# Moving eleven stationary tiles by 32 to 448 bytes inside their slots, in a fused linear-attention and gMLP kernel

## The chip, the core and the metric

The kernel runs on one core of a Trainium2 chip. The metric is the device time of one execution in microseconds (us); the time before is the median of three runs.

## What is computed

The input `x` has 2048 rows of 512. It is normalized by rows, and two branches are added to it:

```python
xn = _layernorm(x, axis=-1)
return x + _A_ref(xn, A_wqkv, A_w_phi, A_wo) + _B_ref(xn, B_w_in, B_w_sp, B_b_sp, B_w_out)

# A: linear attention, 32 heads of 16
qkv = (x @ wqkv)...; pq = q @ w_phi; pk = k @ w_phi            # per head
phi_q = [softmax(pq), softmax(-pq)]; phi_k = [softmax(pk), softmax(-pk)]
kv = phi_k^T v; z = sum_s phi_k
o = (phi_q kv) / (phi_q z + 1e-6);  return o @ wo

# B: gMLP
z = gelu(x @ w_in)                     # 512 -> 1376
z1 = z[..., :688]; z2 = layernorm(z[..., 688:])
g = w_sp @ z2 + b_sp                   # over the 2048 rows
return (z1 * g) @ w_out
```

All arrays are float32.

## The kernel before

The 2048 rows are 16 tiles of 128 (`NT`, index `s`). For exactness with fast matmuls every operand is split into a rounded part and a remainder: ScalarE rounds (`round_h`, line 49), VectorE subtracts (`rest_l`, line 53), and `mm3` (lines 57 to 59) makes three matmuls of each product: high by high, high by low, low by high. The first operand of a matmul is the stationary one: TensorE loads it with a weight load of its own (the engine row PEld in the profile), 128 columns at a time; the second is the moving one, which streams past.

The centered and transposed x of a tile is `xT[s]`: 128 partitions, 2 x 512 values, first the rounded part, then the remainder. It is the stationary operand of all products with x: of `proj` (512 moving columns: wv, and the two halves of wqk, whose matrix is folded with w_phi) and of `zproj`, which `z1_raw` calls for z1 with the weights `w1`, and the z2 stage with `w2` (twice 344 moving columns each). One tile's z1 (12) runs in 512 and 176 columns instead, and so does tile 0's z2. An `xT` tile is read up to the end of the z2 stage, some 150 us or more after it was written.

The stages in order of time: the projections, the softmax features and z1 (to about 216 us; the last z1 tiles, 11 to 15, behind the other projections), z2 (to 276), the gate products `g` (to 480; a Strassen form with moving operands `B` from z2 and stationary operands `A` from w_sp, 344 columns, also through `mm3`), then the output projections `pout`. A scheduler sets the order inside the projection stage; the rest stands as written.

All `xT` tiles come from the pool `xz`: 16 slots, each `SL` = 1408 values long, that is 5632 bytes or eleven times 512. The pool begins 448 bytes past a multiple of 512, and so do the weights `wv`, `wqk`, `w1` and `w2`, whose pieces of one contraction step are 2048 or (padded from 344 to 384 columns) 1536 bytes apart. Of a slot, an `xT` tile takes the first 4096 bytes. Before and after it the slots hold other things (raw weights, `xc`, later `B` and others), at addresses that the change leaves alone. A `B` tile has four blocks of 344 values, 1376 bytes apart, in the same kind of slot; the `A` tiles begin at 448 or 0 past a multiple of 512.

Two places make an `xT` tile: `split_x`, for tiles 1 to 15, and a piece of code of its own for tile 0.

Of the kernel before, what the change touches and what calls it, by code (L numbers as in the profile page):

```python
# [11 lines left out]
F32R = mybir.dt.float32r  # L12
# [7 lines left out]
S, D, H, DH, FH = 2048, 512, 32, 16, 688  # L20
# [21 lines left out]
def mixer(ctx: ExitStack, tc: tile.TileContext, x, x_t, wv, wqkT, phi_bd, wo, w_in, wst, b_r, w_out, out):  # L42
# [4 lines left out]
    def round_h(eng, h, src):  # L47
        if eng is act:
            return act.activation(h, src, AF.Copy).ins  # L49
        return eng.tensor_copy(h, src).ins  # L50

    def rest_l(l, src, h, eng=None):
        return (eng or dve).tensor_tensor(l, src, h.bitcast(F32), op=ALU.subtract).ins  # L53
# [18 lines left out]
    def xz_tile(n, dt, name):  # L72
        return xz.tile([P, SL], dt, tag="xz", name=name)[:, :n]
# [64 lines left out]
    def zproj(ps, s, w, order=(0, 1), wide=False):  # L138

        if ps in (za, kv_ps_p):  # L140
            p = [ps.tile([P, D], F32, tag="z", name="zps") for _ in range(2)]
        else:
            q = ps.tile([P, 2, D], F32, tag="z", name="zps")
            p = [q[:, k] for k in range(2)]
        t = xT[s]
        if wide:
            parts = [(slice(0, 2), slice(LW, FC)), (slice(0, 2), slice(0, LW))]
            dst = [p[k][:, :2 * (f.stop - f.start)].rearrange("p (a b) -> p a b", a=2) for k, (_, f) in enumerate(parts)]
            for (_, f), d in zip(parts, dst):
                for c in range(ND):  # L150
                    cs = slice(c * P, (c + 1) * P)
                    zproj.last = mm3(d, (t[:, 0, cs], t[:, 1, cs]), [v[:, :, c, f] for v in w.both], c == 0, c == ND - 1)
            return list(zip(parts, dst))
        for k, j in enumerate(order):
            for c in range(ND):
                cs = slice(c * P, (c + 1) * P)
                zproj.last = mm3(p[k][:, :FC], (t[:, 0, cs], t[:, 1, cs]), (w[j][0][:, c], w[j][1][:, c]), c == 0, c == ND - 1)
        if ps in (za, kv_ps_p):
            return [((slice(k, k + 1),), p[k][:, :FC].unsqueeze(1)) for k in range(2)]
        return [((slice(0, 2),), q[:, :, :FC])]  # L160
# [7 lines left out]
    def z1_raw(pl, ps, s, bufs, wide=False):  # L168
        z = pl.tile([P, 2, FC], F32, tag="zf", bufs=bufs, name="z1f")
        for k, p in zproj(ps, s, w1, wide=wide):  # L170
            act.activation(z[(slice(None), *k)], p, AF.Copy, scale=r_x[:, s:s + 1])
        act.dma_start(z1_d[s], z.rearrange("p a b -> p (a b)"))

    LAG = 5
    RUNS = (3, 7, 11, 13, 15)
    xT = []
    ctx_w1 = left("w1", 1)
# [17 lines left out]
    with ExitStack() as p0:  # L195
# [60 lines left out]
        def load_win(dst, j):  # L256
            t = zw.tile([P, 4, FC], F32, tag="z2", bufs=2, name="wst_")
            for c in range(ND):
                split_w(dst[0][:, c], dst[1][:, c], w_in[c * P:(c + 1) * P, j * FC:(j + 1) * FC], t[:, c])
# [12 lines left out]
                xt[s] = load_x(s)  # L272

        def split_x(src):
            t = xz_tile(2 * D, F32R, "xT").rearrange("p (a b) -> p a b", a=2)
            xT.append(t)
            rounded.append(round_h(act, t[:, 0], src))
            split_x.last = rest_l(t[:, 1], src, t[:, 0])
            return rounded[-1], split_x.last
# [21 lines left out]
        def centered(s):  # L301
            stats(s)
            nm = neg_mean(s)
            rstd_of(mv_x[:, s], r_x[:, s:s + 1])
            with tc.issue_after(rounded[s - 2]):
                center(s, nm)
            split_x(transposed(s)[0])
# [36 lines left out]
        def proj_v(s):  # L344
            keep_v(s, proj(s, wv_h, wv_l))
# [12 lines left out]
        def add_kv(s, er):  # L358
# [4 lines left out]
            ready.append((v.pop(s), e))  # L363
            if s not in RUNS:
                return
            first = s == RUNS[0]
            with ExitStack() as later:
# [59 lines left out]
        def split_t(pt):  # L427
            i, j = split_x(pt)
            keep(act=i, dve=j)


        t = xz_tile(2 * D, F32R, "xT").rearrange("p (a b) -> p a b", a=2)
        xT.append(t)
        x0, pts = xt.pop(0), []
        for k in range(2):
            pts.append(ps.tile([P, 2, P], F32, tag="mm", name="pt"))
# [14 lines left out]
        p = ps.tile([P, D], F32, tag="mm", name="proj")  # L451
# [7 lines left out]
        p = ps.tile([P, D], F32, tag="mm", name="proj")  # L459
# [18 lines left out]
        p = ps.tile([P, D], F32, tag="mm", name="proj")  # L478
# [19 lines left out]
        ek.append(proj_k(1))  # L498
        keep(pe=proj.last)
        split_x(turned(3))  # L500
        z1_raw(wk, za, 0, 2)
        keep(pe=zproj.last)
# [3 lines left out]
        for s in range(NT):  # L506
# [26 lines left out]
            elif 2 < s < NT - 1:  # L533
                proj_v(s + 1)
            while n1 < s * (NT - LAG) // (NT - 1):
                z1_raw(wk, za, n1, 2)
# [95 lines left out]
    with ExitStack() as p1:  # L632
# [6 lines left out]
        def make_zb():  # L639

            ones_r = tmp1.tile([P, P], F32R, name="ones_r")
            round_h(act, ones_r, ones)
            for k in range(2):
                pz = psk.tile([P, D], F32, tag="kvt", name="pz")
                cs = slice(k * D, (k + 1) * D)
                h, l = (zhl[:, 2 * k + n] for n in range(2))
                round_h(act, h, zacc[:, cs])
                rest_l(l, zacc[:, cs], h)
                pe.matmul(pz, ones_r, h, start=True, stop=False)
                pe.matmul(pz, ones_r, l, start=False, stop=True)  # L650
                dve.tensor_copy(zb[:, cs], pz)
# [13 lines left out]
        for j in range(2):  # L665
            load_win(w2[j], 2 + j)
        for s in range(NT - LAG, NT):
            z1_raw(tmp1, (za, zbp)[s % 2], s, 2, s == NT - LAG + 1)
            if s == NT - LAG + 2:
                make_zb()  # L670
# [67 lines left out]
    for s in range(NT):  # L738
        p = zproj((kv_ps_p, zc, zbp, za)[s % 4], s, w2, (0, 1) if s % 2 == 0 else (1, 0), s == 0)
# [147 lines left out]
    for n in range(NC):  # L887
# [13 lines left out]
        if n % NQ == NQ - 1 and i < NP - 1:  # L901
# [3 lines left out]
            if i in (2, 4):  # L905
                s = i // 2 - 1
                e, t = (gt.tile([P, 2, FU], F32, tag=tag, name=name).rearrange("p k f -> p (k f)")[:, :NF]
                        for tag, name in (("c", "c"), ("z1", "z1t")))
# [12 lines left out]
        if n == NC - 2:  # L921
# [4 lines left out]
            t = xz_tile((KF + 1) * P, F32R, "u1")  # L926
# [156 lines left out]
    p, nxt = {}, dict(enumerate(uT))  # L1083
# [62 lines left out]
```

## Time and profile before

| | |
|---|---|
| median of 3 runs | 616.13 us (615.02 to 616.36) |
| the profiled execution | 618.88 us |
| its span, first to last instruction | 617.1 us |
| granted TensorE clock | 0.997 |
| TensorE busy | 606.7 us |
| VectorE busy | 518.9 us |
| ScalarE busy | 261.3 us |

PE is TensorE's matmuls, PEld its weight loads, DVE is VectorE, ACT ScalarE, POOL GpSimd, SP the engine that issues most transfers. Rows of a group give line, engine, operation, names out<-in, and xcount. A matmul's recorded end is modelled; consecutive matmuls overlap, so that the distance from start to start (called the pace here) is shorter than the recorded duration. In windows, an instruction counts in a window that it touches with any part.

### The profile page before, as it was taken

What the parts mean: (1) busy time and instruction counts of PE and PEld (TensorE: products, weight loads), DVE (VectorE), ACT (ScalarE), POOL (GpSimd) and SP (SyncE); (2) the same over time, 40 slices, a digit from 0 to 9 for tenths busy, and PEclk for the clock granted to TensorE, in tenths of its full rate; (3) what the DMA queues carried; (4) which work ended last, traced back from release to release, by engine and by line L of the source; (5) the groups of instructions that cost most, each with busy time, mean ns of one, the idle gap of its engine ahead of it and who ended that gap; (6) DMA issues with size and microseconds to landing.
All of it is one profiled execution on the core that took longest, in us unless ns stands there. A gap on an engine that the chain in (4) does not pass through costs nothing.

```text
span 617.1 us, 11396 instructions
## 1 busy us (share of the span) xinstructions
PE 606.7 (98%) x4286; PEld 552.5 (90%) x4286; DVE 518.9 (84%) x929; ACT 261.3 (42%) x416; POOL 134.7 (22%) x236
## 2 busy tenths in 40 slices
PE   8999999999999999999999999999999998999996
PEld 6888888888888999999999999999999886777775
DVE  5999999999978588999899897697879889799921
ACT  5653334323523547886444443343345232332221
POOL 4123232232110024452000002001000222143420
PEclk9999999999999999999999999999999998999999
DMA  8557876666447848001463646446466799799782
GB/s 312 191 136 169 224 178 174 158 160 172 125 140 201 287 144 302 2 1 35 151 150 114 199 118 193 129 128 192 135 184 224 202 330 363 216 276 245 191 219 58
DMA packets 58414, 109.95 MB, mean 178 GB/s; under 512 B 12456, under 2 KB 24616, under 8 KB 58120
## 3 DMA queue, kind: packets, MB, share of 16 engines
q1 hardware_dynamic: 43400, 64.96, 34.4%
q0 software_dynamic: 12656, 38.64, 24.9%
q10 hardware_dynamic: 2304, 5.64, 2.4%
q8 instruction: 33, 0.54, 0.4%
q14 instruction: 21, 0.17, 0.1%
HBM read 66.85 MB, written 35.80 MB: 166 GB/s over the span
## 4 chain that ended last, share of the span: by engine, by line
PE 89%; DMA 5%; DVE 3%; issue 2%; SPq 1%; ACT 0%; POOL 0%; POOLq 0%; DVEq 0%
PE g L57 11%; PE g L59 11%; PE g L58 11%; PE proj L58 7%; PE proj L57 7%; PE proj L59 7%; PE zps L59 6%; PE zps L58 6%; PE zps L57 6%; PE pout L57 4%; PE pout L59 4%; PE pout L58 4%; DMA zacc<-e 1%; DMA er<-et 1%; PE kvps L373 1%
## 5 line engine op out<-in xcount | busy, mean ns | idle before, releaser
L57 PE MATMUL g<-B,A 128*128 128x344 f32 x448 | 142.6, 319 | 0.0
L58 PE MATMUL g<-B,A 128*128 128x344 f32 x448 | 142.3, 319 | 0.0
L59 PE MATMUL g<-B,A 128*128 128x344 f32 x448 | 139.4, 319 | 0.0
L57 PEld LDWEIGHTS g<-B,A 128*128 128x128 f32 x448 | 84.0, 188 | 0.3 <-ACT A L49 0.3
L58 PEld LDWEIGHTS g<-B,A 128*128 128x128 f32 x448 | 84.1, 188 | 0.0
L59 PEld LDWEIGHTS g<-B,A 128*128 128x128 f32 x448 | 83.6, 188 | 0.0
L49 ACT ACTIVATE A<-S 128x512 fp32r<-128x512 f32 x64 | 39.2, 628 | 74.3 <-DVE S L622 49.6
L57 PE MATMUL proj<-wqk_h,xT 128*128 128x512 f32 x128 | 50.1, 391 | 0.0
L59 PE MATMUL proj<-wqk_h,xT 128*128 128x512 f32 x128 | 49.8, 389 | 0.0
L58 PE MATMUL proj<-wqk_l,xT 128*128 128x512 f32 x128 | 49.8, 389 | 0.0
L125 ACT ACTIVATE e<-e,r_x 128x1024 f32<-128x1024 f32 x26 | 29.8, 1148 | 42.2 <-DVE e L124 41.2
L53 DVE TENSOR_TENSOR A<-S,A 128x512 fp32r<-128x512 f32 x64 | 42.8, 683 | 3.0 <-ACT A L49 2.8
L49 ACT ACTIVATE A<-wf 128x512 fp32r<-128x512 f32 (+1 forms) x64 | 32.8, 517 | 25.2 <-DMA wf<-in_wst 14.2
L57 PE MATMUL zps<-w1h,xT 128*128 128x344 f32 (+2 forms) x128 | 40.7, 320 | 0.0
L58 PE MATMUL zps<-w1l,xT 128*128 128x344 f32 (+2 forms) x128 | 40.7, 318 | 0.0
L59 PE MATMUL zps<-w1h,xT 128*128 128x344 f32 (+2 forms) x128 | 40.7, 318 | 0.0
L57 PE MATMUL zps<-w2h,xT 128*128 128x344 f32 (+2 forms) x128 | 40.7, 318 | 0.0
L58 PE MATMUL zps<-w2l,xT 128*128 128x344 f32 (+2 forms) x128 | 40.6, 317 | 0.0
L59 PE MATMUL zps<-w2h,xT 128*128 128x344 f32 (+2 forms) x128 | 40.3, 317 | 0.0
L53 DVE TENSOR_TENSOR A<-wf,A 128x512 fp32r<-128x512 f32 (+1 forms) x64 | 34.8, 548 | 4.9 <-ACT A L49 4.8
L128 DVE TENSOR_REDUCE sm<-e 128x64 f32<-128x1024 f32 x26 | 31.1, 1198 | 2.5 <-ACT e L125 2.5
L787 POOL DMA_DIRECT2D z1t<-z_d x16 | 8.7, 552 | 108.1 <-DMA wf<-in_wst 59.6
(222 smaller groups left out, 1436.3 us busy)
## 6 DMA issues: line engine op xcount, KB each, us to landing
wf<-in_wst SPq DMA_DIRECT2D x64, 256.0 KB, 3.3
e_d<-e POOLq DMA_DIRECT2D x16, 544.0 KB, 4.8
et<-e_d SPq DMA_DIRECT2D x16, 544.0 KB, 7.3
z_d<-z1f ACTq DMA_DIRECT2D x16, 344.0 KB, 2.9
z1t<-z_d POOLq DMA_DIRECT2D x16, 344.0 KB, 4.1
zacc<-e POOLq DMA_DIRECT2D x10, 512.0 KB, 4.8
u<-u_d SPq DMA_DIRECT2D x15, 320.0 KB, 5.5
xt<-in_x SPq DMA_DIRECT2D x16, 256.0 KB, 4.0
```

Of the source, the lines that this page charges most:

```text
L49: return act.activation(h, src, AF.Copy).ins
L53: return (eng or dve).tensor_tensor(l, src, h.bitcast(F32), op=ALU.subtract).ins
L57: pe.matmul(dst, ah, bh, start=start, stop=False)
L58: pe.matmul(dst, ah, bl, start=False, stop=False)
L59: return pe.matmul(dst, al, bh, start=False, stop=stop).ins
L125: softmax_pair.last = less, act.activation(e, e, AF.Exp, scale=scale).ins
L128: dve.tensor_reduce(sm, heads(e), axis=AX.X, op=ALU.add)
L373: i = pe.matmul(kv_acc[k:k + QP, m // 4], vs[:, m * QP:(m + 1) * QP], e[:, m * HP:(m + 1) * HP], start=first and m < 4 and len(ready) == n ...
L787: pool.dma_start(t[:, k, :FH], z1_d[2 * i + k])
```

## The change

From the fifth on (tiles 4 to 14; tile 15 by 0), each `xT` tile begins `o` values further up in its slot, so 4 * `o` bytes. The slots, all other tiles and the order of instructions stay as they are.

```diff
     LAG = 5
+    XO = (0, 0, 0, 0, 32, 64, 96, 16, 48, 80, 112, 8, 32, 64, 96, 0)
+
+    def xT_tile():
+        o = XO[len(xT)]
+        xT.append(xz_tile(2 * D + o, F32R, "xT")[:, o:].rearrange("p (a b) -> p a b", a=2))
+        return xT[-1]
+
     RUNS = (3, 7, 11, 13, 15)
     xT = []
...
         def split_x(src):
-            t = xz_tile(2 * D, F32R, "xT").rearrange("p (a b) -> p a b", a=2)
-            xT.append(t)
+            t = xT_tile()
             rounded.append(round_h(act, t[:, 0], src))
             split_x.last = rest_l(t[:, 1], src, t[:, 0])
             return rounded[-1], split_x.last
...
-        t = xz_tile(2 * D, F32R, "xT").rearrange("p (a b) -> p a b", a=2)
-        xT.append(t)
+        t = xT_tile()
         x0, pts = xt.pop(0), []
```

## The prediction

> **What bounds the kernel now.** I read the page's engine totals and its chain first.
>
> ```profile
> span 617.1 us, 11396 instructions
> PE 606.7 (98%) x4286; PEld 552.5 (90%) x4286; DVE 518.9 (84%) x929; ACT 261.3 (42%) x416; POOL 134.7 (22%) x236
> PE 89%; DMA 5%; DVE 3%; issue 2%; SPq 1%; ACT 0%; POOL 0%; POOLq 0%; DVEq 0%
> ```
>
> TensorE is busy for 98% of the span and makes 89% of the chain that ended last. That is an average, so next comes busy time by stage: the projections (40 to 196 us), the z2 stage (217 to 276), the gate products g (276 to 480) and the output stage.
>
> ```profile
> core 0: us, PE busy (x) PEld busy (x) DVE busy (x) ACT busy (x) POOL busy (x), PEclk, DMA share, GB/s
> 40.00:196.00 156.00, 156.00 (x1204) 135.47 (x1206) 145.88 (x231) 56.60 (x74) 41.74 (x71) 1.00 0.64 168
> 217.00:276.00 59.00, 59.00 (x383) 58.50 (x383) 52.02 (x107) 43.66 (x66) 25.40 (x42) 1.00 0.32 111
> 276.00:480.00 204.00, 204.00 (x1300) 203.74 (x1299) 174.78 (x365) 89.55 (x157) 16.72 (x30) 1.00 0.52 150
> 480.00:617.00 137.00, 129.53 (x827) 103.86 (x825) 104.30 (x160) 38.86 (x64) 39.27 (x61) 0.99 0.82 234
> ```
>
> In the two stages that read xT, TensorE has no idle time at all, and VectorE has slack (145.88 of 156, 52.02 of 59). So what matters there is the pace at which matmuls follow each other: a nanosecond more on each is a nanosecond more at the end. The granted clock is 1.00 in each of these stages and takes no part.
>
> **The change part by part.** The built program has the same instructions in the same order on every engine, the same waits, and every tile in the same place; only the start of twelve xT tiles inside their slots differs (eleven in fact, the twelfth by 0). So no DMA, no queue and no buffer is touched. Three kinds of instruction see the new addresses: ScalarE's rounding and VectorE's remainder that write xT, and the weight loads of TensorE that read it (xT is the stationary operand).
>
> *The writers.* VectorE's remainders and ScalarE's roundings of xT, and for comparison the remainders of A (durations as minimum, median and maximum in ns, then first and last start):
>
> ```profile
> L53 DVE TENSOR_TENSOR xT<-xc,xT x7: 679/680/682, 62.4 to 132.2; 128x512 fp32r<-128x512 f32 x7
> L53 DVE TENSOR_TENSOR A<-S,A x64: 643/682/694, 218.6 to 476.9; 128x512 fp32r<-128x512 f32 x64
> L49 ACT ACTIVATE xT<-xc x7: 613/614/624, 60.1 to 130.9; 128x512 fp32r<-128x512 f32 x7
> ```
>
> The first row's operands all start at the same remainder by 512 bytes (448). In the second the sources and targets start at 0, 64, 320 and 448 in several pairings, and the same work takes the same 682 ns in the median. I put the writers at nothing; the bound is the spread of the second row, 643 to 694, so -39 to +12 ns on 11 instructions, under 0.5 us, and it is covered by TensorE, which runs through these stages without a wait. If that cover were gone, it would be those 0.5 us at most.
>
> *The weight loads.* How many there are:
>
> ```profile
> L57 PE MATMUL proj<-wqk_h,xT x128: 389/389/481, 16.4 to 190.0; 128*128 128x512 f32 x128
> L57 PE MATMUL proj<-wv_h,xT x64: 388/389/502, 6.8 to 178.2; 128*128 128x512 f32 x64
> L57 PE MATMUL zps<-w1h,xT x128: 243/316/497, 25.4 to 216.0; 128*128 128x344 f32 x120, 128*128 128x176 f32 x4, 128*128 128x512 f32 x4
> L57 PE MATMUL zps<-w2h,xT x128: 275/316/418, 216.6 to 275.5; 128*128 128x344 f32 x120, 128*128 128x176 f32 x4, 128*128 128x512 f32 x4
> ```
>
> Each row is one of the three products of `mm3` (L57, L58, L59). Over 16 tiles that is (128+64)*3/16 = 36 matmuls of 512 columns and (128+128)*3/16 = 48 of 344 for each tile; eleven moved tiles make 396 and 528. Each has its own weight load.
>
> Now the pace. One table of windows in which TensorE never pauses: 512-column projections; z1 of tiles 13 and 14; z2; and g. Behind it, from the groups by tile, the recorded durations (minimum, median, maximum in ns) of a product of that z1 and of one of g, to hold against the 316 ns of z2 above.
>
> ```profile
> core 0: us, PE busy (x), PEclk, DMA share, GB/s
> 62.50:70.60 8.10, 8.10 (x37) 1.00 0.75 166
> 205.00:212.20 7.20, 7.20 (x48) 1.00 0.95 307
> 222.00:275.90 53.90, 53.90 (x353) 1.00 0.28 96
> 290.00:470.00 180.00, 180.00 (x1147) 1.00 0.54 155
> ...
> L58 PE MATMUL zps<-w1l,xT x16: 321/321/321, 205.0 to 212.1; 128*128 128x344 f32 x16
> L57 PE MATMUL g<-B,A x403: 314/319/428, 289.9 to 479.6; 128*128 128x344 f32 x135
> ```
>
> A matmul is recorded for about two paces, so some two of each count (one at 512 columns) began before the window. The z2 row gives 53.90/351 = 153.6 ns; g, with the same 344 columns and a weight load of the same size, 180.00/1145 = 157.2 ns. The 512-column row gives 8.10/36 = 225 ns, to within one matmul in 36. The recorded durations tell the same: 316 ns in z2, 319 in g.
>
> What differs between z2 and g that this change could touch? In the built program all of xT, w1, w2, wv and wqk start 448 bytes past a multiple of 512, and every piece of them a whole multiple of 512 further: stationary and moving operand always start at the same remainder. In g the moving B pieces start at 64, 192, 320 and 448 and the stationary A pieces at 0 or 448, so they mostly differ. The rows where the one stage goes over into the other without a pause:
>
> ```profile
> 275.48 0.32 PE L57 MATMUL zps<-w2h,xT 128*128 128x344 f32 x1
> ...
> 275.78 0.31 PE L59 MATMUL zps<-w2h,xT 128*128 128x344 f32 x1
> 275.94 0.32 PE L57 MATMUL g<-B,A 128*128 128x344 f32 x1
> 276.09 0.32 PE L58 MATMUL g<-B,A 128*128 128x344 f32 x1
> 276.25 0.32 PE L59 MATMUL g<-B,A 128*128 128x344 f32 x1
> 276.41 0.32 PE L57 MATMUL g<-B,A 128*128 128x344 f32 x1
> ```
>
> Three matmuls take 0.46 us up to 275.94 and 0.47 right behind it: the slower pace begins with the first mixed pair. My reading: the weight load of the next matmul reads at the same time as this matmul's moving operand, and off the common remainder the two get in each other's way for some 4 ns. The change takes xT off that remainder, so z1 and z2 of the moved tiles should run at g's pace.
>
> Price for 344 columns: 157.2 - 153.6 = 3.6 ns each; the lower bound is none (g may be slow for another reason), the upper one about 4.5 ns. Of the 528 matmuls, three groups drop out. Tile 12's z1 runs as 12 of 512 and 12 of 176 columns (24). Tiles 13 and 14 run their z1 already at 7.20/46 = 156.5 ns (321 recorded) before the change (48), a point that returns below. And z1 of tiles 10 and 11 (48) lies beside a wait that is not TensorE's own (rows of the chain: start, duration; the last is from the waits):
>
> ```profile
> 195.06 7.02 DMA zacc<-e
> 202.10 0.64 ACT zhl L49
> 202.76 0.69 DVE zhl L53
> PE pz L650 <- DVE zhl L53: 0.3, 1, 0.3
> ```
>
> From 195 to 203.5 us the chain runs over the zacc DMA, and TensorE sits 0.3 us for it; 48 * 3.6 = 0.17 us more work there only shortens that wait. Left are 528 - 24 - 48 - 48 = 408 matmuls: 408 * 3.6 = 1.5 us.
>
> Price for 512 columns: no row shows a mixed pair of this width, so I bound it. Lower end: the undisturbed 225 to 227 ns of the window above, that is nothing; a gain has no room where the streams already run free. Upper end: the pace just after an interruption.
>
> ```profile
> 37.92 0.48 PE L57 MATMUL proj<-wqk_h,xT 128*128 128x512 f32 x1
> 38.24 0.40 PE L58 MATMUL proj<-wqk_l,xT 128*128 128x512 f32 x1
> 38.47 0.40 PE L59 MATMUL proj<-wqk_h,xT 128*128 128x512 f32 x1
> 38.70 0.40 PE L57 MATMUL proj<-wqk_h,xT 128*128 128x512 f32 x1
> 38.94 0.39 PE L58 MATMUL proj<-wqk_l,xT 128*128 128x512 f32 x1
> ...
> 40.09 0.39 PE L57 MATMUL proj<-wqk_h,xT 128*128 128x512 f32 x1
> 40.32 0.39 PE L58 MATMUL proj<-wqk_l,xT 128*128 128x512 f32 x1
> 40.55 0.39 PE L59 MATMUL proj<-wqk_h,xT 128*128 128x512 f32 x1
> ```
>
> After transposes broke the stream, three take 38.94 - 38.24 = 0.70 us, 233 each, some 7 to 8 ns over; from 40.09 to 40.55 it is 230 each, and in the window from 62.5 it is down to 225 to 227. [...] So between 0 and 8 I take 1.8 ns, half of what I gave the narrow one: 396 * 1.8 = 0.7 us.
>
> Sum: 1.5 + 0.7 = 2.2 us. Nothing downstream absorbs it: the g stage starts when z2 is done and is itself without a pause, and the output stage follows g. The profiled execution took 618.88 us, a span of 617.1 and 1.8 around it, so it should become about 621.1. The three timed runs have their median at 616.13, 2.75 below the profiled one; on them I forecast 616.1 + 2.2 = 618.3 us. A measurement of this kernel can tell about 0.2% (1.2 us) from no change.
>
> **The rivals.**
>
> *Nothing happens.* Weight load and moving operand do not meet, and g is slower for a reason of its own. For it: tiles 13 and 14 run z1 at 156.5 ns on operands of equal remainder, so the slow pace exists without a mixed pair; something else, such as how the stream was entered after the pause at 204.5 us, must set it there. Against it: the pace changes at 275.94 with no pause at all. Time 616.1 us, and anything up to +1.2 belongs here too: if only half of the 3.6 ns comes about and the wide matmuls recover fully, it is 0.7 us. This is the case on the other side, not slower; it decides if the recorded duration of z2's matmuls stays at 316 ns on moved tiles. [...]
>
> *Both widths stay in the disturbed pace.* The wide matmuls cannot recover, since the cause is there again with every load: 396 * 8 = 3.2 us, and 408 * 4.5 = 1.8 us, together 5.0: 621.1 us. For it: the 38.24 to 38.94 rows. Against it: the same rows a microsecond later.
>
> *Faster.* Common remainders are themselves what costs something, and spreading them frees it. The shortest matmul recorded in g took 314 ns, 2 less than z2's 316: 504 * 2 = 1.0 us over the narrow ones, and the slow z1 of tiles 13 and 14 would give 48 * 2.9 = 0.14. Together 1.1 us: 615.0 us. It decides only if nearly every narrow matmul falls to the shortest one's pace. Against it: that is the best of 403 in a row whose median is 319, so mixed pairs are mostly the slower ones.
>
> **How the numbers follow.** Forecast 0.50 (its own range 617.4 to 619.7), nothing 0.29, both widths disturbed 0.14, faster 0.07. Slower by over 0.2% is 0.50 + 0.14 = 0.64, within 0.2% 0.29, faster 0.07. The predicted time is the forecast's, 618.3. For 8 in 10 the range takes in nearly all of the second case and most of the third: 615.4 to 621.1 us.
>
> **What the profile would show.** If right: in the window of z2, matmuls of tiles 0 to 3 and 15 keep a median of 316 ns and those of tiles 4 to 14 show 318 to 321; z2, with 264 matmuls of moved tiles, lasts 264 * 3.6 = 0.95 us longer; the 512-column rows lie between 389 and 391; VectorE's and ScalarE's rows on xT are unchanged; g and the output stage keep their lengths and start later. Wrong if z2 keeps its length (nothing), if the projections between 62 and 190 us grow by over 2 us (disturbed), or if any single offset, such as the 32 bytes of tile 11, which is no multiple of 64 and has no row here, costs far more than the others.

## The result, and the profile after

The changed kernel takes 620.03 us (median of five runs, 619.08 to 622.49) against 616.36 (615.02 to 617.12) before: a ratio of 1.0061, 95% interval 1.0037 to 1.0085. It is slower by some 3.7 us; 2.2 were forecast. The page of the changed kernel begins:

```profile
span 617.5 us, 11396 instructions
PE 609.7 (99%) x4286; PEld 553.7 (90%) x4286; DVE 519.8 (84%) x929; ACT 263.6 (43%) x416; POOL 134.5 (22%) x236
```

The spans of the two profiled executions (617.1 and 617.5) do not show the loss, since the first trace of before was long in a part that the change does not reach: from the first g matmul to the end it took 341.2 us, this one 337.7. (The difference lies in the output stage. In the first trace TensorE waited 2.5 us there for the DMA `er<-et`, and the granted clock was 0.51 from 520.9 to 524.4 us; the changed kernel's trace has neither.) Up to the first g matmul it is 275.9 us before and 279.8 now, 3.8 us more, which is what the timed runs say too. So the two traces are compared by pace, not by span. Busy time of TensorE in stretches of the changed kernel: the wqk projections of tile 5 (moved by 256 bytes), of tile 7 (64 bytes); z2 of the unmoved tiles up to 3, of the moved ones, of tile 15 (offset 0); g.

```profile
core 0: us, PE busy (x), PEclk, DMA share, GB/s
62.41:65.13 2.72, 2.72 (x13) 1.00 0.80 206
84.50:87.29 2.79, 2.79 (x14) 1.00 0.75 87
225.00:234.50 9.50, 9.50 (x64) 1.00 0.14 56
234.60:276.00 41.40, 41.40 (x266) 1.00 0.31 110
276.00:279.70 3.70, 3.70 (x26) 1.00 0.00 0
290.00:470.00 180.00, 180.00 (x1147) 1.00 0.53 151
```

TensorE is busy throughout and its clock is full: only the pace differs. The 264 matmuls of the moved tiles in z2 take 41.40 us, 156.8 ns each, against 153.6 by the same kind of count before; g has not changed (1147 records in the same 180 us). The same groups by recorded duration (min/median/max ns), tile 5 and tile 7 in one product of the projections, then z2 in the same three stretches, and the two writers of xT:

```profile
L57 PE MATMUL proj<-wqk_h,xT x4: 389/389/389, 62.4 to 64.5; 128*128 128x512 f32 x4
L57 PE MATMUL proj<-wqk_h,xT x4: 394/394/395, 84.5 to 86.6; 128*128 128x512 f32 x4
L58 PE MATMUL zps<-w2l,xT x21: 316/316/316, 224.7 to 234.2; 128*128 128x344 f32 x21
L58 PE MATMUL zps<-w2l,xT x88: 314/318/324, 234.7 to 275.7; 128*128 128x344 f32 x88
L58 PE MATMUL zps<-w2l,xT x8: 321/321/321, 276.2 to 279.5; 128*128 128x344 f32 x8
L53 DVE TENSOR_TENSOR xT<-xc,xT x7: 680/682/687, 62.3 to 133.4; 128x512 fp32r<-128x512 f32 x7
L49 ACT ACTIVATE xT<-xc x7: 611/614/620, 60.0 to 132.2; 128x512 fp32r<-128x512 f32 x7
```

Tile 5 is as fast as before and tile 7 is not. Tile 15, which is not moved, is as slow as any (321 where it had 316), and the writers are where they were. The distances between the starts of consecutive matmuls are finer than the windows. Averaged over the 24 of wqk and the 24 of z2 of a tile:

| moved by, bytes (tile) | wqk, 512 columns, ns | z2, 344 columns, ns |
|---|---|---|
| 0 (the same tiles before) | 226.7 | 153.3 |
| 32 (11) | 233.4 | 155.6 |
| 64 (7) | 233.1 | 157.7 |
| 128 (4) | 233.2 | 156.8 |
| 192 (8) | 229.5 | 156.0 |
| 256 (5) | 227.1 | 157.8 |
| 320 (9) | 233.2 | 157.9 |
| 384 (6) | 233.0 | 157.0 |
| 448 (10) | 229.7 | 156.0 |

For the wide matmuls offsets that differ by 256 bytes behave alike (64 and 320, 128 and 384, 192 and 448, 0 and 256). For the narrow ones 256 looked as bad as 64, which the first experiments had to explain.

### The profile page after: what moved, and what is told of

It reads as the page before. It is cut to its first block, busy times and chain, and to the rows that moved or that the text cites. A ratio compares the mean times of both kernels' runs of the same rounds, so it can differ in the third digit from the quotient of the medians.

```text
span 617.5 us, 11396 instructions
## 1 busy us (share of the span) xinstructions
PE 609.7 (99%) x4286; PEld 553.7 (90%) x4286; DVE 519.8 (84%) x929; ACT 263.6 (43%) x416; POOL 134.5 (22%) x236
## 4 chain that ended last, share of the span: by engine, by line
PE 86%; DMA 6%; DVE 4%; issue 2%; SPq 1%; POOL 0%; ACT 0%; DVEq 0%; POOLq 0%
PE g L57 11%; PE g L59 11%; PE g L58 11%; PE proj L58 7%; PE proj L57 7%; PE proj L59 7%; PE zps L58 6%; PE zps L57 6%; PE zps L59 6%; PE pout L57 3%; PE pout L59 3%; PE pout L58 3%; DMA zacc<-e 1%; PE kvps L379 1%; DMA et<-e_d 1%
```

## The experiments

The theory to be tested: the cost lies in how the weight load and the moving operand start relative to each other. Its rivals: moving a tile costs as such; the place of the stationary tile itself counts; a slow pace is inherited from what ran before. Unless said otherwise only the table of offsets is edited.

**All tiles by 512 bytes.**

```diff
-    XO = (0, 0, 0, 0, 32, 64, 96, 16, 48, 80, 112, 8, 32, 64, 96, 0)
+    XO = (0,) * 4 + (128,) * 12
```

> All tiles from the fifth on are moved by 512 bytes, a whole period. Theory (what costs is the start of the weight load relative to the start of the moving operand, by its remainder): nothing is lost, 616.4 us, ratio 1.000 within 0.002; 512-column projections of tiles 4 to 15 at 226.7 ns from start to start, z2 at 153.3. Rival (any move out of the slot's start costs, by the writers or by the distance of the tiles from each other): as the change or a little more, ratio 1.005 to 1.007, 233 and 157 ns.

Measured: 616.11 us, ratio 0.9992 (0.9972 to 1.0012). Busy time in the projections and in z2:

```profile
62.50:70.40 7.90, 7.90 (x36) 1.00 0.72 158
222.00:275.00 53.00, 53.00 (x348) 1.00 0.28 97
```

53.00 us for some 346 matmuls, 153.2 each: as before. Moving a tile costs nothing as such; the remainder does.

**All tiles by 256 bytes.**

```diff
+    XO = (0,) * 4 + (64,) * 12
```

> All tiles from the fifth on are moved by 256 bytes. In the changed kernel tile 5, at 256 bytes, kept 226.7 ns in its 512-column projections but 157.8 in z2. Theory, with a period of 256 bytes for the wide and of 512 for the narrow matmuls: projections at 226.7 ns; narrow ones at 157.8, 408 uncovered and 24 of tile 15 times 4.4 ns = 1.9 us, so 618.3 us, ratio 1.003. Rival (the narrow pace is only inherited from how the stream was entered, and tile 5 took it over from its neighbours): the stream enters freely here, so narrow ones at 153.3 too, ratio 1.000.

Measured: 616.13 us, ratio 1.0003 (0.9987 to 1.0020). The first row is z2 of the moved tiles, the second z1 of tiles 13 and 14:

```profile
L58 PE MATMUL zps<-w2l,xT x96: 316/316/316, 231.8 to 275.5; 128*128 128x344 f32 x96
L58 PE MATMUL zps<-w1l,xT x12: 316/316/316, 205.6 to 210.6; 128*128 128x344 f32 x12
```

Here the theory as I had put it, with a period of 512 bytes for narrow matmuls, was wrong and the rival right: at 256 bytes the narrow ones are free too. Tile 5 in the changed kernel (157.8 ns in z2) had only taken the slow pace over from tile 4; here the three products of z2 have medians of 316 ns, 53.60 us for some 350 matmuls or 153.1 each. The second row is a by-product: the z1 of tiles 13 and 14, slow throughout in before (321 ns), here ran at 153.3 ns from their fifth matmul on. That is worth some 0.2 us, too little for the timed runs to tell.

**All tiles by 64 bytes.**

```diff
+    XO = (0,) * 4 + (16,) * 12
```

> All tiles from the fifth on are moved by 64 bytes, the worst remainder seen (tile 7: 233.1 ns wide, 157.7 narrow). Theory: 432 wide matmuls (12 tiles) times 6.4 ns = 2.8 us, 432 narrow ones times 4.4 = 1.9 us, together 4.7: 621.1 us, ratio 1.0075, above the change's 1.006. Rival (it is the variety of remainders, each tile differing from its neighbour, that throws the stream out of step): with all tiles alike the stream settles, projections back at 227, ratio 1.000 to 1.003.

Measured: 621.05 us, ratio 1.0074 (1.0059 to 1.0089), against the 621.1 of the theory. Projections, then z2:

```profile
72.50:80.50 8.00, 8.00 (x37) 1.00 0.88 229
236.00:277.00 41.00, 41.00 (x262) 1.00 0.33 108
```

41.00 us for 260 matmuls are 157.7 ns each; by the distances of starts the wide matmuls of each tile from 4 to 15 average 233.3, where nothing interrupts them. So a common start of all tiles does not let the stream settle; the cost is there on each matmul. The digits of the time agree in part by luck: z1 of tiles 4 to 9 runs at 159.8 ns, not at the 157.7 that the theory had for every narrow matmul, so the same difference of 64 bytes has one pace in z1 and another in z2.

**Twelve other remainders.**

```diff
+    XO = (0, 0, 0, 0, 128, 1, 4, 12, 24, 40, 56, 64, 72, 88, 120, 384)
```

> One look: tiles 4 to 15 moved by 512, 4, 16, 48, 96, 160, 224, 256, 288, 352, 480 and 1536 bytes, to see the pace of each remainder. Theory (period of 256 bytes for the wide matmuls): tiles 4, 11 and 15 (512, 256 and 1536 bytes) at 226.7 ns, all others at 229 to 234, 4 and 16 bytes either free, if what counts is a coarser unit, or like 64 bytes, 233. Rival (only multiples of 64 bytes matter, a smaller move is worse because it cuts a unit of memory in two): tiles 5 to 7 (4, 16, 48 bytes) clearly above 234 ns.

One execution, 622.09 us. Distances of starts in the wqk projections: 227.0 ns at 512 bytes, 232.5 at 4, 230.3 at 16, 232.2 at 48, 234.0 at 96, 233.1 at 160, 233.0 at 224, 228.0 at 256, 233.2 at 288, 233.8 at 352, 233.0 at 480, 229.0 at 1536. The wv projections of the tile at 16 bytes ran at 226.7 and its z2 at 153.5, so 16 bytes cost nothing, and its 230.3 are behind slow neighbours (as the 228.0 and 229.0 at 256 and 1536 bytes may be; tile 15 at offset 0 showed 230.1 in the changed kernel). Four bytes cost nearly as much as 64, and so do 48; neither the theory nor the rival had that order. The group rows of z2 at 512 and at 4 bytes:

```profile
L58 PE MATMUL zps<-w2l,xT x8: 316/316/317, 234.0 to 237.2; 128*128 128x344 f32 x8
L58 PE MATMUL zps<-w2l,xT x8: 317/320/322, 237.7 to 241.0; 128*128 128x344 f32 x8
```

**The difference or the place?** The kernel before, without its pad at the start:

```diff
-    cst.tile([P, 8], F32, name="pad")
```

> One look at the kernel before without its 32-byte pad at the start: xT, wv, wqk and w1 all begin 32 bytes lower, together; w2 stays, so in z2 all sixteen tiles are 32 bytes off their moving operand. Theory (the difference of the two starts counts): projections and z1 as before, 226.7 and 153.3 ns; z2 slow for all tiles, 155.6 to 158 ns, about 336 * 4 = 1.3 us longer. Rival (the place of the stationary tile itself counts, 448 past a multiple of 512 being the good one): projections and z1 slow too, 233 and 156 to 158 ns, some 3 us more.

One execution, 620.93 us. The projections, where both operands moved by 32 bytes together, and z2, where one did:

```profile
L57 PE MATMUL proj<-wqk_h,xT x8: 389/389/389, 62.3 to 67.0; 128*128 128x512 f32 x8
L57 PE MATMUL zps<-w2h,xT x115: 318/318/318, 221.8 to 275.7; 128*128 128x344 f32 x115
```

The place of the tile does not count, the difference does: projections and z1 kept 226.7 and 153.3 ns, z2 went to 156.7 on every tile. (The single time is further up than z2 accounts for: it has 360 matmuls of 344 columns, not the 336 that I had counted, so 360 * 3.4 = 1.2 us. The rest lies behind the first g matmul, where this execution took 342.6 us. TensorE waited there 3.6 us for the DMA `f<-q_d`, 0.3 in the changed kernel's trace. The pad also lies ahead of tiles of the later stages; one run does not tell whether that or chance made the wait.)

**One tile by 64 bytes.**

```diff
+    XO = (0, 0, 0, 0, 16, 0, 0, 0, 0, 0, 4, 0, 0, 0, 0, 0)
```

> One look: only tile 4 is moved, by 64 bytes, and tile 10, by 16 (16 bytes was free in the sweep). Theory (a narrow stream that was thrown out stays out, whatever comes next, until a tile with another start lets it back; a wide one recovers by itself): z2 of tiles 4 to 9 at 157.7 ns though 5 to 9 lie as before; tile 10 back at 153.5, tiles 11 to 15 at 153.3; in the projections only tile 4 (233 ns) and the few matmuls behind it are slow. Rival (each tile pays for its own start alone): z2 of tile 4 at 157.7, tiles 5 to 9 at 153.3.

One execution, 619.93 us. Z2 of tiles 1 to 3; of 5 to 8, which lie as before; of tile 10, at 16 bytes; of 11 to 15. Then z1 of tile 4, and the next z1, of tile 5:

```profile
L58 PE MATMUL zps<-w2l,xT x22: 316/316/316, 222.1 to 231.9; 128*128 128x344 f32 x22
L58 PE MATMUL zps<-w2l,xT x32: 320/320/320, 236.2 to 250.9; 128*128 128x344 f32 x32
L58 PE MATMUL zps<-w2l,xT x8: 318/321/323, 255.1 to 258.4; 128*128 128x344 f32 x8
L58 PE MATMUL zps<-w2l,xT x40: 321/321/321, 258.9 to 277.3; 128*128 128x344 f32 x40
L57 PE MATMUL zps<-w1h,xT x8: 321/321/322, 95.2 to 98.6; 128*128 128x344 f32 x8
L57 PE MATMUL zps<-w1h,xT x2: 316/316/316, 104.6 to 105.0; 128*128 128x344 f32 x2
```

In z2 one moved tile makes all narrow matmuls behind it slow, 157.8 ns to the end of the stage, though eleven of these twelve tiles lie where they did or within 16 bytes of it. The wide ones do recover: tile 4's projections ran at 233, those of the unmoved tiles at 226.7 to 228.6. And wide ones let the narrow stream back in: z1 of tile 4 ran at 159.5 ns, then came 24 wide matmuls of unmoved tiles, and z1 of tile 5 ran at 153.3. My expectation that the tile at 16 bytes would let the stream back in was wrong (157.1, then 157.8 again); in the sweep it did so, behind a tile that was slow at 156.5.

**The kernel before once more.**

> One look at the kernel before, unchanged, for a second trace: projections to z2 as in the first (226.7, 153.3 ns; 275.9 us from the span's start to the first g matmul, within 1 us). From there to the end the first trace took 341.2 us and the changed kernel's 338.0, though nothing is changed there; if that difference is chance of one execution, this one is at 338 to 339.

Measured: 617.24 us, span 615.5. The first g matmul starts at 276.1 us, within 0.2 us of the first trace, and from there to the end it takes 339.4; the two traces of before, that of the change and those at 512, 256 and 64 bytes lie between 337.7 and 341.2 in this part, which none of them changes. So the spread is chance of an execution, wider than I expected; in the first trace it is the wait of 2.5 us and the stretch at a clock of 0.51 named above.

**Is g slow for the same reason?** All its pairs are brought to one remainder by 256, by reading only B operands of one kind and moving one set of A tiles. This kernel leaves out the right blocks of z2 in half of the products, so its output is not that of the computation:

```diff
-    mid.enter_context(right("pad", 1)).tile([P, P - 8], F32, name="pad")
+    mid.enter_context(right("pad", 1)).tile([P, P - 8 - 48], F32, name="pad")
...
     zw = ctx_zw.__enter__()
+    zw.tile([P, 48], F32, name="pad2")
...
+                bn = {"B21": "B22", "T3": "T1", "T4": "T2"}.get(bn, "B22" if bn == "B11" and k else bn)
                 (ah, al), (bh, bl) = ops[an], B[2 * q + k][bn]
```

> The gate stage with all pairs brought to one remainder. Of the B operands only those lying 192 past a multiple of 256 are used, so half of the products take the wrong block of z2 (this leaves the right output out; the number and size of matmuls stay); the second set of A tiles is moved up by 192 bytes, so that both sets lie at 192 too, and a pad keeps w2 in its place. Theory (g's 157 ns are the same cost that the change brought to z2): g at 153.3 to 154 ns, 1344 * 3.5 = 4.7 us less, 611.6 us, ratio 0.992. Rival (g is slow for a reason of its own, its switching between PSUM tiles or the freshly written A tiles): g stays at 157, ratio 1.000. Third: the stream is thrown out by some pause within g and cannot come back, 153.3 at first and 157.7 after it.

Measured: 617.11 us, ratio 1.0008 (0.9984 to 1.0032). No gain, and the trace says why: the third possibility. Products of g up to 293.7 us and from 296 on; TensorE's waits; the timeline between:

```profile
L58 PE MATMUL g<-B,A x39: 316/316/316, 275.9 to 293.4; 128*128 128x344 f32 x39
L57 PE MATMUL g<-B,A x389: 317/320/321, 295.8 to 479.9; 128*128 128x344 f32 x195
...
PE g L57 <- ACT A L49: 0.4, 1, 0.4
...
294.00 0.31 PE L59 MATMUL g<-B,A 128*128 128x344 f32 x1
294.75 0.42 PE L57 MATMUL g<-B,A 128*128 128x344 f32 x1 [0.44 <-ACT A L49]
295.01 0.32 PE L58 MATMUL g<-B,A 128*128 128x344 f32 x1
```

For its first 120 matmuls g ran at 153.3 ns, a pace it never holds in before. Then it waited 0.44 us for one A tile from ScalarE, and from there to the end of the stage every stretch of 10 us averages 157.8, with the same remainders. The 1166 matmuls that start between 296 and 480 us take 4.4 ns more each, 5.1 us together. That the wait brought this on is read from where the pace changes, once in one trace; no run takes the wait away.

## Why the prediction was right, and where it was off

The direction and the range held, and so did the core of my reading: off the common remainder the same matmuls follow each other more slowly (on average 157.0 ns for 153.3 in z2, 231.3 for 226.7 in the projections), and nothing else changes. Against 616.36 us the measured 620.03 lies inside the range of 615.4 to 621.1, but above the forecast's own 617.4 to 619.7, and the 3.7 us are about as near to the 5.0 of the rival with both widths disturbed as to the 2.2 of the forecast. *The pace of TensorE as the bound*: right; the distances of starts of all matmuls that read xT add up to 4.0 us more, the first g matmul starts 3.8 us later, and the timed runs show 3.7. *The writers at nothing*: right, 682 against 680 ns and 614 against 614. *Narrow matmuls*: forecast 3.6 ns each. The moved tiles show 3.64 in z2 (0.96 us for 264, the forecast said 0.95). In z1, tiles 4 to 9 lost 4.6 ns (0.67 us instead of 0.52), and tiles 13 and 14 nothing, as I had assumed. That 3.64 comes so near to 3.6 is luck, as is shown below.

*The term that was mis-sized is the wide matmuls.* I took 1.8 ns between bounds of 0 and 8, half of the narrow price, from a stream that came back from 233 ns to 225 to 227 after transposes. No run shows 1.8 as the price of a mixed wide pair. In the experiment with one tile the wide stream did come back behind tile 4, from 233 ns to between 226.7 and 228.6, on tiles at the common remainder; with every tile 64 bytes off it stayed at 233.3. The moved tiles' projections lost 4.6 ns on average, 1.8 us in all instead of 0.7: 6.5 at five remainders, 3 at two, none at 256 bytes. That the bounds were right and the value within them was not is the whole of the 1.1 us between 0.7 and 1.8. By my own sign for that rival, the projections between 62 and 190 us growing by over 2 us, it was the rival that came true here: from the first wqk matmul of tile 5 to the first z1 matmul of tile 10 it is 128.2 us before and 130.8 after (some 0.8 of it from z1), and the rows that I expected at 389 to 391 ns show medians of 392 to 396 on every moved tile but those at 256 bytes. The rival with both widths disturbed came nearer in this point, at 8 ns; all tiles by 64 bytes, at 233.3 ns (6.6 more), are that rival almost as priced.

*Unmoved tiles* were forecast to stay at 316 ns. They did up to tile 3 of z2, but tile 15 went to 321, and z1 of tiles 2 and 3 and the wide matmuls of tile 15 rose too: together 0.3 to 0.4 us that the sum did not have. The pace I had noted as "slow without a mixed pair", z1 of tiles 13 and 14, was the clue. By the distances of starts it is 157.7 ns, not the 156.5 that I had from a window, so the pace that the experiments show as a state: the narrow stream mostly stayed in it once entered (157.8 ns to the end of z2 behind one moved tile, and over the 184 us of g from 296 us on), until wide matmuls came between (159.5 ns ahead of them and 153.3 behind, in the experiment with one tile).

*What I took from the step at 275.94 us* was half right. The pace does change at the first mixed pair, from 152 to 154 ns between starts ahead of it to 156 to 159 on the first four behind it. But that g stays slow is not the sum of its mixed pairs: in the last experiment it stayed slow without any. The slow state itself costs 4.4 to 4.5 ns. My 3.6 is a mean over g's pairs, which run in before at 155.8 to 158.1 ns by the difference of their starts, and the 3.64 is a mean over the moved tiles, from 2.3 to 4.6; the two mixtures need not have agreed.

*The cover of tiles 10 and 11* by the zacc transfer (0.17 us) does not show: TensorE's wait there is 0.3 us in both traces, and what tiles 10 and 11 lost in z1, 0.12 us, is too little to be told from them.

Against the rival "nothing happens", at 0.29: 64 bytes of difference between the two operands cost 4.4 ns on a narrow matmul of z2 and 6.6 on a wide one, 256 and 512 cost none. That two reads get in each other's way was my inference from the addresses. The traces show only that a weight load (188 ns recorded) begins with the matmul before its own, and the paces; no run shows that reads meet, or which two they would be.

No version beat the kernel before. The one that the experiments point to, g at 153.3 ns throughout, would need all its operands at one remainder and no wait in the stage, or something that lets the stream back after one; that was not tried.

## What to carry to other kernels

Where TensorE runs without idle time, compare the distance between the starts of equal matmuls from stage to stage: some 4 ns on each did not show in the busy share (53.90 of 53.90 us in z2 before, 41.40 of 41.40 after) and were 0.6% here. Compare where the stationary operand and the moving one start: in this kernel they ran at 226.7 and 153.3 ns at the same remainder by 256 bytes, and at 233.3 and 157.7 with 64 bytes between. It was the difference that counted: the projections kept 226.7 ns when both operands moved by 32 bytes, and a pad less in front of one of them cost z2 3.4 ns a matmul. And look at what a stream of matmuls has come from: one tile 64 bytes off left the narrow ones of z2 behind it at 157.8 ns, and as it seems one wait of 0.44 us did so to g; behind 24 wide ones z1 was back at 153.3.

## What was not expected of the hardware

In the last experiment a stream of 344-column matmuls showed two paces at the same remainders, 153.3 and 157.8 ns, and kept the slow one from 296 to 480 us, behind a single wait of 0.44 us. It did not stay everywhere: with all tiles moved by 256 bytes, z1 of tile 13 was back at 153.3 ns four matmuls after an interruption. A stream of 512 columns returned to 226.7 ns within some ten matmuls (in before, behind the transposes that end at 46.5 us). Off the common remainder a third narrow pace showed: with all tiles moved by 64 bytes, z1 of tile 4 ran at 160.0 ns, z2 at 157.8. In before, twelve 176-column and twelve 512-column matmuls of tile 0 between z1 and z2 stand between the two paces: z1 of tile 14 at 157.8 ahead of them, z2 at 153.3 behind. A difference of 16 bytes cost nothing on a fresh stream (226.7 and 153.5 ns), one of 4 bytes 5.8 ns on a wide matmul and one of 48 bytes 5.5; the runs do not say why.
